# All eleven tiles of an expert layer through a seven-product scheme

## The chip, the cores and the metric

The kernel runs on one core of a Trainium2 chip. The metric is the device time of one execution in microseconds. A core has TensorE (matmuls, results into PSUM, of which the program uses eight banks of 512 fp32 columns), VectorE, ScalarE, GpSimd and SyncE, which here issues all transfers. The profile calls them PE, DVE, ACT, POOL and SP; PEld is the loading of a matmul's stationary operand.

## The reference

Three layers follow each other; everything is fp32. Attention has 4 x 8 heads over 576 positions of 64 features and keeps the 32 largest scores of a row. Its output is a matrix x of 2304 tokens and 512 features. A dense layer computes g = h cos(h) with h = x w_in (2048 wide) and then g w_out. The last layer mixes eight experts:

```
logits = x @ w_gate;  P = exp(logits - max)
8 times: P /= row sums; P /= column sums; P *= N / E
for e in 8 experts:
    h  = max(x @ w1[e], 0)          # 2304 x 512 @ 512 x 1024
    out += P[:, e:e+1] * (h @ w2[e])  # 2304 x 1024 @ 1024 x 512
```

## The kernel before

**Precision.** The matmuls of this part work in the type float32r. A matrix is split into a high part (ScalarE, a copy into that type) and a low part (VectorE or GpSimd, the difference), `split_cols`. A product then takes three matmuls: high x high, high x low, low x high (`mm3`, lines 504 to 510).

**Order.** Every operation is given to a planner (`put`) with its engine, an estimated cost, what it reads and what it writes. The planner (`listed`, line 245 on) goes through time: when an engine is free it takes, of the operations whose inputs are ready by the estimates, the one that was put first (within this part of the program). The order so found for each engine is then fixed; on the chip each engine works in that order and waits by semaphores. The estimate for a matmul of n columns is `mm_ns`, n/2.4 + 3 ns.

**Stages.** The first seven token tiles of 128 ("fill") go through the experts early, beside attention; their expert outputs are kept in memory and summed up at the end (`sum_fill`, 56 steps). The other eleven tiles (RT = 11) are the subject. Their dense layer (`moe1`) runs in three parts of 512, 512 and 384 tokens. `moe1` makes first-layer blocks ("in", twelve matmuls) and, seven blocks later, starts second-layer blocks; hidden values pass through rings of three buffers (hs, rr). At its end `keep_raw` (parts one and two) copies the result from the banks y0 to y3 to the buffer acc, splits it and computes the logits; `keep_parts` (part three) only splits it.

**The last stage** goes over 8 experts and 4 quarters j of the 1024 hidden features (two blocks of 128 hidden features each): 32 passes. The first matmul of a pass, 2 x 256 features halves by 2 x 128 hidden features by two halves of the tokens, is a 2 x 2 block product. For the first eight tiles it is made with seven products instead of eight (`mixed_first`, a scheme of Strassen's kind): `weight_mix` forms the sums of weight blocks on GpSimd (S1 to S4), `combine` once forms the differences of token blocks on VectorE (T1 to T4) and splits all seven operands (th, tl). Each product is six matmuls of 512 columns into one of four banks (s, y3, h, g, in turn); two are copied to SBUF by ScalarE, five sums are made by VectorE and two by GpSimd in SBUF; the results go through `gates`: the high part of relu by ScalarE, the low part by VectorE. The other three tiles (384 tokens) take plain matmuls, 24 of 384 columns (`plain_first`). Then each of the eleven tiles has six second matmuls of 512 columns into a bank of y0 to y2 (`mixed_second`), and VectorE multiplies by the gate's column and adds to acc. Blocks are put so that the tiles of one block come behind the first products of the next block. The gate normalisation (`sinkhorn`) is put before the first pass; it uses the bank t.

Of the kernel before, what the change touches and what calls it, by code (L numbers as in the profile page):

```python
# [10 lines left out]
F32 = mybir.dt.float32  # L11
F32R = mybir.dt.float32r
# [332 lines left out]

def act_ns(n, psum=False, ap=False):
    return (51.0 if psum else 93.0) + n / 1.2 + (93.0 if ap else 0.0)
# [10 lines left out]
def fused_kernel(tc, kq, vv, w_in, w_out, w_gate, w1, w2, out, B=4):  # L358
# [14 lines left out]
    LEAD, FILL, MIXED = 3, 7, 8  # L373
    AHEAD = (2, 1, 1)
    RT = NTT - FILL
    NR = NT - (FILL + MIXED) * 128
# [127 lines left out]
    def mm3(o, ob, ah, al, bh, bl, n, start, stop, bufs):  # L504
# [5 lines left out]
        put("PE", 3 * mm_ns(n), emit, bufs, [ob])  # L510
# [343 lines left out]
    def keep_raw(xb, i0):  # L854


        def done(p):
            n, pb = p.n, p.h()
            for d in range(4):
                h2, l2 = gh_r(), gl_r()  # L860
                yb, yv = p.y(d)
                r2, rb = (lambda d=d: xb.ap[:, i0 + d, :n]), (xb, i0 + d, i0 + d + 1)
                put("ACT", act_ns(n, psum=True), lambda yv=yv, r2=r2: A_.activation(r2(), yv(), AF.Copy), [yb], [rb])
                split_cols((h2, lambda h2=h2: h2.ap[:, :n]), (l2, lambda l2=l2: l2.ap[:, :n]), (rb, r2), n, eng=eng_w)
                put("PE", 2 * mm_ns(n), logits(pb, lambda h2=h2: h2.ap[:, :n], lambda l2=l2: l2.ap[:, :n], d, n), [wg, h2, l2], [pb])
            keep_logits(pb, p.n0, n)

        return done

# [16 lines left out]
    def gates(v, vb, n, g_r, psum):  # L886

        gh, gl = g_r()
        put("ACT", act_ns(n, psum=psum), lambda: A_.activation(gh.ap[:, :n], v(), AF.Relu), [vb], [gh])
        put("DVE", dve_ns(n), lambda: V.scalar_tensor_tensor(gl.ap[:, :n], v(), 0.0, gh.ap[:, :n].bitcast(F32), op0=ALU.max, op1=ALU.subtract), [vb, gh], [gl])  # L890
        return gh, gl

    def fill(e, t0, k, h_ring):
# [10 lines left out]
        for f in range(NF2):  # L904
# [7 lines left out]
            pend.append((f, *gates(lambda pb=pb: pb.ap[:, :n], pb, n, lambda: (gh_r(), gl_r()), True)))  # L912
# [56 lines left out]
    def combine(x2, th, tl):  # L969


        for c in range(2):
            x = lambda i: ((x2, i, i + 1), lambda: x2.ap[:, i, :])
            b11, b21, b12, b22 = x(c), x(c + 2), x(c + 4), x(c + 6)
            t1, t2 = x(8), x(9)
            t3, t4 = ((b, lambda b=b: b.ap) for b in (st_r(), st_r()))
            for o, p, q in ((t1, b12, b11), (t2, b22, t1), (t3, b22, b12), (t4, b21, t2)):
                put("DVE", dve_ns(512), lambda o=o, p=p, q=q: V.tensor_tensor(o[1](), p[1](), q[1](), op=ALU.subtract), [p[0], q[0]], [o[0]])
            for k, v in ((B11, b11), (B21, b21), (B22, b22), (T1, t1), (T2, t2), (T3, t3), (T4, t4)):
                iv = (k * 2 + c, k * 2 + c + 1)  # L980
                split_cols(((th, *iv), lambda k=k, c=c: th.ap[:, k, c, :]), ((tl, *iv), lambda k=k, c=c: tl.ap[:, k, c, :]), v)
# [21 lines left out]
    def mixed_first(A, th, tl, mix_r, g_r):  # L1003

        banks = Cycle([ps_s, ps_y[3], ps_h, ps_g])

        def product(a, b):
            bank = banks()
# [3 lines left out]
            def emit():  # L1012
                for c in range(2):
                    s = slice(s0 + c * 128, s0 + c * 128 + 128)
                    bh, bl = th.ap[:, b, c, :], tl.ap[:, b, c, :]
                    T_.matmul(bank.ap, h.ap[:, s], bh, start=c == 0, stop=False)
                    T_.matmul(bank.ap, h.ap[:, s], bl, start=False, stop=False)
                    T_.matmul(bank.ap, l.ap[:, s], bh, start=False, stop=c == 1)

            put("PE", 6 * mm_ns(512), emit, [h, l, (th, b * 2, b * 2 + 2), (tl, b * 2, b * 2 + 2)], [bank])  # L1020
            return bank, lambda: bank.ap

        bufs = [mix_r() for _ in range(4)]
        spot = lambda i: ((bufs[i // 2], i % 2 * 512, i % 2 * 512 + 512), lambda: bufs[i // 2].ap[:, i % 2 * 512 : i % 2 * 512 + 512])

        def copy(i, x):
            o = spot(i)
            put("ACT", act_ns(512, psum=True), lambda: A_.activation(o[1](), x[1](), AF.Copy), [x[0]], [o[0]])
            return o

        def plus(i, x, y, eng="DVE"):
            o = spot(i)
            f, cost = (V, dve_ns(512)) if eng == "DVE" else (G_, pool_ns(512))
            put(eng, cost, lambda: f.tensor_tensor(o[1](), x[1](), y[1](), op=ALU.add), [x[0], y[0]], [o[0]])
            return o

        def gate(x):
            return gates(x[1], x[0], 512, g_r, False)

        p1 = copy(0, product(A11, B11))  # L1040
        u = plus(1, product(S2, T2), p1)
        p5 = copy(2, product(S1, T1))
        v = plus(3, product(S3, T3), u)
        w = plus(4, u, p5, "POOL")
        c11 = gate(plus(5, product(A12, B21), p1))
        c21 = gate(plus(6, product(A22, T4), v))
        c22 = gate(plus(2, v, p5, "POOL"))
        c12 = gate(plus(7, product(S4, B22), w))
        return (c11, c21), (c12, c22)

    def plain_first(A, xh, xl, n, g_r):
        g = []
        for i, bank in ((0, ps_g), (1, ps_y[3])):
            h, l = A[i]
            for c in range(4):
                s = slice(c * 128, c * 128 + 128)
                iv = (c * n, c * n + n)
                mm3(lambda bank=bank: bank.ap[:, :n], bank, lambda h=h, s=s: h.ap[:, s], lambda l=l, s=s: l.ap[:, s], lambda c=c: xh.ap[:, c, :], lambda c=c: xl.ap[:, c, :],
                    n, c == 0, c == 3, [h, l, (xh, *iv), (xl, *iv)])
            g.append(gates(lambda bank=bank: bank.ap[:, :n], bank, n, g_r, True))  # L1060
        return (tuple(g),)
# [3 lines left out]
    def mixed_second(acc, t0, k, g, e, j, wo):  # L1065
        for t in range(k):
            y, T = y_r(), t0 + t
            c = slice(t % 4 * 128, t % 4 * 128 + 128)
            for i in (0, 1):
                gh, gl = g[t // 4][i]  # L1070
                oh, ol = wo[i]
                mm3(lambda y=y: y.ap, y, lambda gh=gh, c=c: gh.ap[:, c], lambda gl=gl, c=c: gl.ap[:, c], lambda oh=oh: oh.ap, lambda ol=ol: ol.ap,
                    512, i == 0, i == 1, [oh, ol, gh, gl])
            a, av = (acc, T, T + 1), lambda T=T: acc.ap[:, T, :]
# [10 lines left out]
            if e == NE - 1 and j == 3:  # L1085
                r = (FILL + T) * 128
                dma(lambda r=r: out[r : r + 128, :], av, 1 << 18, [a])

# [77 lines left out]
    th = buf("ph2", [128, 7, 2, 512], F32R, "th")  # L1166
    tl = buf("ph2", [128, 7, 2, 512], F32R, "tl")
    xrh = buf("ph2", [128, 4, NR], F32R, "xrh")
    xrl = buf("ph2", [128, 4, NR], F32R, "xrl")
    acc = buf("ph2", [128, RT, DM], F32, "acc")  # L1170
# [3 lines left out]
    moe1(Part(n0 + 512, three, keep_raw(acc, 0)), 4)  # L1174
    moe1(Part(n0 + 1024, three, keep_raw(acc, 4)), 4)
    moe1(Part(n0 + 1536, three, keep_parts(xrh, xrl), NR), 4)
# [65 lines left out]
```

## Time and profile before

| | |
|---|---|
| median of 3 runs | 2364.43 us (2361.56 to 2368.71) |
| profiled execution | 2365.81 us, span of its instructions 2364.0 us |
| mean granted TensorE clock | 0.998 |
| busy share of the span | PE 99%, PEld 82%, DVE 77%, ACT 56%, POOL 53% |
| instructions | 34301, of them 11487 matmuls |
| transfers | 242.28 MB, mean 102 GB/s |

The busy share of an engine is a mean over stages with different limits. In the timeline a row has the start, the duration, the engine, the line of the program, the operation, output and inputs by the program's names, and the shape; a bracket gives the idle time of the engine just before and what ended it. Matmuls are pipelined, so their durations overlap; how long one holds TensorE is read from start to start. "x4" in a row means four merged instructions.

### The profile page before, as it was taken

The numbers are of one execution on the slowest core, as the hardware profiler recorded it, in microseconds if no ns is written. First come the engines' busy times: TensorE is split into PE (matmuls) and PEld (weight loads), VectorE is DVE, ScalarE is ACT, GpSimd is POOL, SyncE is SP. The second block draws the span as 40 slices with busy tenths as digits, with TensorE's granted clock in tenths as the row PEclk, the third lists the DMA queues.
The fourth block names the chain that finished last, engine by engine and source line by source line (L and its number), as shares of the span: only waits on it lengthen the run. The fifth ranks groups of instructions, "written<-read, shape, count | busy, mean of one in ns | idle before, by whom it ended". The sixth has DMA issues, their size and how long they took to land.

```text
span 2364.0 us, 34301 instructions
## 1 busy us (share of the span) xinstructions
PE 2331.9 (99%) x11487; PEld 1932.1 (82%) x11487; DVE 1815.7 (77%) x3340; ACT 1333.3 (56%) x2688; POOL 1260.4 (53%) x1352
## 2 busy tenths in 40 slices
PE   9999999999899999999999999999999999999999
PEld 7655989898677888888888897888888888888887
DVE  7991999999869999999177796876666666666665
ACT  5884888888787777777477675222232222222221
POOL 6982987888876666665401036433333344444440
PEclk9999999999999999999999999999999999999999
DMA  7661654555333333433443332122222221111101
GB/s 222 204 182 40 188 163 141 171 158 169 118 86 94 120 120 120 120 100 95 126 123 108 117 116 65 41 76 77 85 77 80 77 66 36 36 36 36 36 23 49
DMA packets 152464, 242.28 MB, mean 102 GB/s; under 512 B 14624, under 2 KB 61808, under 8 KB 152288
## 3 DMA queue, kind: packets, MB, share of 16 engines
q1 hardware_dynamic: 152288, 240.10, 33.7%
q8 instruction: 90, 1.47, 0.3%
q14 instruction: 86, 0.70, 0.1%
HBM read 208.18 MB, written 31.87 MB: 102 GB/s over the span
## 4 chain that ended last, share of the span: by engine, by line
PE 83%; DVE 7%; POOL 4%; ACT 2%; DMA 2%; issue 2%; SPq 0%; POOLq 0%; ACTq 0%; DVEq 0%
PE y L506 11%; PE y L508 11%; PE y L507 11%; PE g L506 3%; PE g L508 3%; PE g L507 3%; PE t L606 3%; PE h L508 2%; PE h L506 2%; PE h L507 2%; PE y L517 2%; PE y L518 2%; PE t L632 2%; PE y L521 2%; PE s L578 1%
## 5 line engine op out<-in xcount | busy, mean ns | idle before, releaser
L481 POOL TENSOR_TENSOR wlo<-raw,whi 128x512 fp32r<-128x512 f32 x336 | 443.4, 1325 | 141.6 <-ACT whi L479 110.8
L594 DVE MAX8 m<-wk 128x8 f32<-128x576 f32 x432 | 317.7, 749 | 2.7
L1084 DVE SCALAR_TENSOR_TENSOR acc<-y,P,acc 128x512 f32<-128x512 f32 x308 | 229.3, 748 | 103.5 <-PE y L508 103.2
L479 ACT ACTIVATE whi<-raw 128x512 fp32r<-128x512 f32 x416 | 258.0, 626 | 82.5 <-PE y L508 30.4
L593 DVE MATCH_REPLACE8 wk<-m,wk 128x576 f32<-128x576 f32 x288 | 214.1, 744 | 1.9
L506 PE MATMUL y<-whi,gh 128*128 128x512 f32 x448 | 181.1, 404 | 0.0
L508 PE MATMUL y<-whi,gl 128*128 128x512 f32 x448 | 176.3, 394 | 0.0
L506 PE MATMUL y<-gh,xh 128*128 128x512 f32 x450 | 175.9, 391 | 0.1
L507 PE MATMUL y<-wlo,gh 128*128 128x512 f32 x448 | 175.7, 392 | 0.0
L508 PE MATMUL y<-gh,xl 128*128 128x512 f32 x450 | 175.1, 389 | 0.0
L507 PE MATMUL y<-gl,xh 128*128 128x512 f32 x450 | 175.1, 389 | 0.0
L588 ACT ACTIVATE sc<-s 128x288 f32<-128x288 f32 x288 | 116.6, 405 | 36.2 <-PE s L582 20.6
L606 PE MATMUL t<-ident,ex 128*128 128x128 f32 (+1 forms) x720 | 127.3, 275 | 8.0 <-DVE atl L625 3.4
L596 ACT ACTIVATE ex<-sc,m 128x576 f32<-128x576 f32 x144 | 111.1, 772 | 27.0 <-DVE m L594 25.7
L601 POOL TENSOR_SCALAR ex<-ex,m 128x576 f32<-128x576 f32 x144 | 110.8, 770 | 27.6 <-DVE m L600 24.2
L606 PEld LDWEIGHTS t<-ident,ex 128*128 128x128 f32 (+1 forms) x720 | 84.0, 134 | 49.4 <-issue 10.6
L590 DVE MAX8 m<-sc 128x8 f32<-128x576 f32 x144 | 107.5, 747 | 18.8 <-ACT sc L588 18.7
L624 ACT ACTIVATE ath<-t 64x128 fp32r<-64x128 f32 (+3 forms) x272 | 104.2, 395 | 29.0 <-PE t L606 26.1
L597 ACT ACTIVATE ex<-ex,m 128x576 f32<-128x576 f32 x144 | 111.5, 774 | 6.9 <-POOL m L595 2.3
L593 DVE MATCH_REPLACE8 wk<-m,sc 128x576 f32<-128x576 f32 x144 | 106.9, 743 | 0.1
L506 PEld LDWEIGHTS y<-gh,xh 128*128 128x128 f32 x450 | 84.5, 188 | 18.6 <-DVE acc L1080 0.8
L508 PE MATMUL y<-gh,gl 128*128 128x512 f32 x254 | 99.5, 392 | 0.0
(378 smaller groups left out, 7047.2 us busy)
## 6 DMA issues: line engine op xcount, KB each, us to landing
raw<-in_w_dram SPq DMA_DIRECT2D x384, 256.0 KB, 2.7
kq<-in_kq_dram SPq DMA_DIRECT2D x40, 576.0 KB, 4.0
raw<-win_d SPq DMA_DIRECT2D x64, 256.0 KB, 3.0
raw<-wout_d SPq DMA_DIRECT2D x64, 256.0 KB, 2.7
y_d<-st SPq DMA_DIRECT2D x56, 256.0 KB, 3.0
raw<-y_d SPq DMA_DIRECT2D x56, 256.0 KB, 2.7
d_raw<-in_w_in_dram SPq DMA_DIRECT2D x16, 512.0 KB, 5.4
d_raw<-in_w_out_dram SPq DMA_DIRECT2D x16, 512.0 KB, 3.7
```

Source lines behind the costliest of these rows:

```text
L479: put("ACT", act_ns(n), lambda: A_.activation(hv(), rv(), AF.Copy), [rb], [hb])
L481: put(e, c, lambda: f.tensor_tensor(lv(), rv(), hv().bitcast(F32), op=ALU.subtract), [rb, hb], [lb])
L506: T_.matmul(o(), ah(), bh(), start=start, stop=False)
L507: T_.matmul(o(), ah(), bl(), start=False, stop=False)
L508: T_.matmul(o(), al(), bh(), start=False, stop=stop)
L588: put("ACT", act_ns(288, psum=True), lambda c=c: A_.activation(sc.ap[:, c], o(), AF.Copy), [ps_s], [(sc, c.start, c.stop)])
L593: put("DVE", 669, lambda r=r, src=src: V.match_replace(wk.ap, mc(8 * r, 8), src.ap, LOWEST), [src, (m, 8 * r, 8 * r + 8)], [wk])
L594: put("DVE", 669, lambda r=r: V.max(mc(8 * r + 8, 8), wk.ap), [wk], [(m, 8 * r + 8, 8 * r + 16)])
L596: put("ACT", act_ns(S, ap=True), lambda: A_.activation(ex.ap, sc.ap, AF.Prelu, scale=-1.0, bias=mc(31), alpha=TINY), [sc, (m, 24, 32)], [ex])
L597: put("ACT", act_ns(S, ap=True) + 93.0, lambda: A_.activation(ex.ap, ex.ap, AF.Exp, scale=-0.125 / TINY, bias=mc(32), accum_out=mc(33)), [ ...
L606: T_.transpose(pt()[:p, c - c0, :], ex.ap[:, c * 128 : c * 128 + p], ident.ap)
L1084: put("DVE", 663, lambda y=y, av=av, pcol=pcol: V.scalar_tensor_tensor(av(), y.ap, pcol(), av(), op0=ALU.mult, op1=ALU.add), [y, P, a], [a])
```

## The change

All eleven tiles now go through the seven-product scheme, as two operand sets: one of N1 = 384 columns (six tiles) and one of N2 = 320 (five tiles). `plain_first` is gone. Sums are kept in PSUM: product two adds to the bank of product one after that was copied out, product five adds to the same bank, and so on, so that three copies and three VectorE sums (with a PSUM output) remain and GpSimd makes none; gates read PSUM. In the second set each result is gated in two pieces, of 256 and 64 columns. `mixed_first` and `mixed_second` are now generators that are advanced in turn: one product, one tile of the half before. A fifth bank, t, joins the ring of banks from the second expert on. The gate buffers of a pass are all six of their ring. The first operand set is formed before the third part of the dense layer, the second after it; the third part's result is copied in three pieces into acc. The chunks for the first weights are now the four of the dense layer's input. The gate normalisation is put behind the first pass. The expert sums of the fill tiles are taken two in a pass, not four. The planner's estimate for matmuls of this stage is `mx_ns`, n/2.4 + 13.3 ns.

```diff
+def mx_ns(n):
+    return n / 2.4 + 13.3
...
+    N1, N2 = 384, 320
...
-    def keep_raw(xb, i0):
+    def keep_raw(xb, places):
...
-                r2, rb = (lambda d=d: xb.ap[:, i0 + d, :n]), (xb, i0 + d, i0 + d + 1)
-                put("ACT", act_ns(n, psum=True), lambda yv=yv, r2=r2: A_.activation(r2(), yv(), AF.Copy), [yb], [rb])
-                split_cols((h2, lambda h2=h2: h2.ap[:, :n]), (l2, lambda l2=l2: l2.ap[:, :n]), (rb, r2), n, eng=eng_w)
+                for s0, m, k in places:
+                    k += d * (N1 + N2)
+                    put("ACT", act_ns(m, psum=True), lambda yv=yv, s0=s0, m=m, k=k: A_.activation(xb.ap[:, k : k + m], yv()[:, s0 : s0 + m], AF.Copy), [yb], [(xb, k, k + m)])
+                put("ACT", act_ns(n, psum=True), lambda yv=yv, h2=h2: A_.activation(h2.ap[:, :n], yv(), AF.Copy), [yb], [h2])
+                put("DVE", dve_ns(n), lambda yv=yv, h2=h2, l2=l2: V.tensor_tensor(l2.ap[:, :n], yv(), h2.ap[:, :n].bitcast(F32), op=ALU.subtract), [yb, h2], [l2])
...
-    def combine(x2, th, tl):
+    def combine(th, tl, x2, p0, n):
...
-            t1, t2 = x(8), x(9)
-            t3, t4 = ((b, lambda b=b: b.ap) for b in (st_r(), st_r()))
+            ta, tb = hs_r(), rr_r()
+            t1, t2, t3, t4 = (((b, k, k + n), lambda b=b, k=k: b.ap[:, k : k + n]) for b in (ta, tb) for k in (0, 512))
...
-    def mixed_first(A, th, tl, mix_r, g_r):
-
-        banks = Cycle([ps_s, ps_y[3], ps_h, ps_g])
+    banks = Cycle([ps_s, ps_y[3], ps_h, ps_g])
+
+    def mixed_first(A, th, tl, n, temps, dest):
...
+            put("PE", 6 * mx_ns(n), emit, [h, l, (th, b * 2, b * 2 + 2), (tl, b * 2, b * 2 + 2)], [bank])
...
+        def plus(out, bank, x):
+            put("DVE", dve_ns(n), lambda: V.tensor_tensor(out.ap[:, :n], bank.ap[:, :n], x[1](), op=ALU.add), [bank, x[0]], [out])
+
+        def gate(i, bank):
+            for (gh, gl), k, s0, m in dest[i]:
+                gates(lambda s0=s0, m=m: bank.ap[:, s0 : s0 + m], bank, m, gh, gl, k, psum=True)
+
+        X, Z = banks(), banks()
+        product(X, A11, B11)
+        p1 = copy(0, X)
+        yield
+        product(Z, S1, T1)
+        yield
+        product(X, S2, T2, True)
+        u = copy(1, X)
+        yield
+        Y = banks()
+        product(Y, A12, B21)
+        plus(Y, Y, p1)
+        gate(0, Y)
+        yield
+        product(X, S3, T3, True)
+        v = copy(2, X)
+        W = banks()
+        plus(W, Z, v)
+        gate(3, W)
+        yield
+        product(Z, S4, B22, True)
+        plus(Z, Z, u)
+        gate(2, Z)
+        yield
+        product(X, A22, T4, True)
+        gate(1, X)
+        yield
...
+    moe1(Part(n0 + 512, three, keep_raw(acc, [(0, 512, 0)])), 4)
+    moe1(Part(n0 + 1024, three, keep_raw(acc, [(0, 512, 4 * N)])), 4)
+    combine(*t1, acc, 0, N1)
+    moe1(Part(n0 + 1536, three, keep_raw(acc, [(0, 192, 512), (192, 64, 4 * N + 640), (256, 128, 4 * N + 512)]), NR), 4)
     whi_r.bufs, wlo_r.bufs = ring
-    combine(acc, th, tl)
-    sinkhorn()
-    chunks = list(zip(more[:1] + whi_r.bufs + gh_r.bufs, more[1:] + wlo_r.bufs + gl_r.bufs))
-    chunks += [(View(xh, i), View(xl, i)) for i in range(4)]
+    combine(*t2, acc, N1, N2)
+    chunks = [(View(xh, i), View(xl, i)) for i in range(4)]
+    chunks += zip(more[:1] + whi_r.bufs + gh_r.bufs, more[1:] + wlo_r.bufs + gl_r.bufs)
...
+    second, sums = iter(()), sum_fill()
     for e in range(NE):
+        if e == 1:
+            banks.bufs.append(ps_t)
         for j in range(4):
             A = weight_mix(e, j, wa_r, mix_r)
             wo = [split_weight(w2[e, f], dst=w2_r()) for f in (j, j + 4)]
...
+            g = [[g_r() for _ in range(2)] for _ in range(3)]
+            temps = [mix_r() for _ in range(3)]
+
+            firsts = (
+                mixed_first(A, *t1, N1, temps[:2], [[(g[i // 2][i % 2], 0, 0, N1)] for i in range(4)]),
+                mixed_first(A, *t2, N2, temps[2:], [[(g[2][i % 2], i // 2 * 256, 0, 256), (g[0][i % 2], 384 + i // 2 * 64, 256, 64)] for i in range(4)]),
+            )
+            tiles = (
+                [(t, g[t // 4], t % 4 * 128) for t in (0, 1, 2, 4, 5, 6)],
+                [(3, g[2], 0), (8, g[2], 128), (9, g[0], 384), (7, g[2], 256), (10, g[2], 384)],
+            )
+            for first, tile_list in zip(firsts, tiles):
+                for _ in first:
+                    next(second, None)
+                for _ in second:
+                    pass
+                second = mixed_second(acc, tile_list, e, j, wo)
             if e == j == 0:
-                for part in [plain(), mixed()]:
-                    mixed_second(acc, *part)
-                continue
...
+                sinkhorn()
             if e:
-                for _ in range(4):
+                for _ in range(2):
                     next(sums, None)
```

## Rows read from the trace of the kernel before

**Rows 1.** The page's chain that ended last: share of the span by engine.

```profile
PE 83%; DVE 7%; POOL 4%; ACT 2%; DMA 2%; issue 2%; SPq 0%; POOLq 0%; ACTq 0%; DVEq 0%
```

**Rows 2.** Busy time by stretch: stretch, length, busy us (instructions) by engine, granted clock, transfers.

```profile
core 0: us, PE busy (x) PEld busy (x) DVE busy (x) ACT busy (x) POOL busy (x), PEclk, DMA share, GB/s
1366.00:1391.00 25.00, 25.00 (x146) 25.00 (x145) 24.06 (x37) 21.08 (x39) 19.30 (x5) 1.00 0.37 113
1413.00:1440.00 27.00, 24.29 (x127) 21.79 (x126) 19.71 (x27) 16.04 (x30) 15.26 (x12) 0.94 0.38 110
1440.00:1520.00 80.00, 78.94 (x371) 65.04 (x370) 61.48 (x132) 31.90 (x56) 44.27 (x37) 1.00 0.15 41
1520.00:2360.00 840.00, 840.00 (x3861) 714.86 (x3859) 540.41 (x765) 227.05 (x396) 316.54 (x274) 1.00 0.19 56
```

**Rows 3.** Timeline of TensorE: ends of two blocks of a pass, and one 18 passes later.

```profile
1810.54 0.39 PE L1016 MATMUL s<-th,whi 128*128 128x512 f32 x1
...
1820.06 0.39 PE L506 MATMUL y<-gh,xh 128*128 128x512 f32 x1
...
1824.14 0.33 PE L506 MATMUL g<-xrh,whi 128*128 128x384 f32 x1
...
1828.32 0.39 PE L506 MATMUL y<-gh,gh 128*128 128x512 f32 x1
...
2340.86 0.33 PE L506 MATMUL g<-xrh,whi 128*128 128x384 f32 x1
```

**Rows 4.** Timeline of TensorE in attention: matmuls of 320 columns.

```profile
709.16 0.31 PE L634 MATMUL t<-atl,vs 128*128 128x320 f32 x1
...
709.89 0.31 PE L632 MATMUL t<-ath,vs 128*128 128x320 f32 x1
```

**Rows 5.** Timeline of a pass: from a bank's last matmul to its readers.

```profile
1817.34 0.39 PE L1016 MATMUL y<-th,whi 128*128 128x512 f32 x1
1817.54 0.69 DVE L1034 TENSOR_TENSOR rr<-s,hs 128x512 f32<-128x512 f32 x1 [0.67 <-PE s L1018]
...
1818.33 0.63 ACT L889 ACTIVATE gh<-rr 128x512 fp32r<-128x512 f32 x1 [2.91 <-DVE rr L1034]
...
2342.96 0.33 PE L506 MATMUL y<-xrh,whi 128*128 128x384 f32 x1
...
2343.22 0.49 ACT L889 ACTIVATE xh<-g 128x384 fp32r<-128x384 f32 x1 [3.78 <-PE g L508]
...
2343.75 0.56 DVE L890 SCALAR_TENSOR_TENSOR xl<-g,xh 128x384 fp32r<-128x384 f32 x1 [1.94 <-ACT xh L889]
```

**Rows 6.** Chain that ended last, in time: from a VectorE difference to its matmul.

```profile
1431.71 0.04 issue
```

**Rows 7.** Groups of VectorE instructions from 1600 to 2200: busy us, mean ns, idle before.

```profile
L1084 DVE SCALAR_TENSOR_TENSOR acc<-y,P,acc 128x512 f32<-128x512 f32 x231 | 171.8, 748 | 71.6 <-PE y L508 71.3
L481 DVE TENSOR_TENSOR gl<-raw,gh 128x512 fp32r<-128x512 f32 x41 | 37.2, 947 | 0.0
```

**Rows 8.** Timeline of the entry to the last stage, TensorE and VectorE.

```profile
1424.42 0.45 PE L517 MATMUL y<-gh,whi 128*128 128x384 f32 x1 [0.80 <-ACT gh L479]
1424.70 0.34 PE L518 MATMUL y<-gh,wlo 128*128 128x384 f32 x1
...
1431.15 1.94 DVE L879 TENSOR_TENSOR xrl<-y,xrh 128x384 fp32r<-128x384 f32 x4
```

**Rows 9.** Timeline of the third part's start: VectorE, ScalarE, TensorE and GpSimd.

```profile
1370.64 1.78 DVE L978 TENSOR_TENSOR acc<-acc 128x512 f32<-128x512 f32 x1
...
1372.95 0.68 DVE L978 TENSOR_TENSOR st<-acc 128x512 f32<-128x512 f32 x1
...
1374.60 0.99 ACT L479 ACTIVATE gh<-rr 128x384 fp32r<-128x384 f32 x2 [0.91 <-DVE rr L731]
...
1375.62 0.33 PE L517 MATMUL y<-gh,ch 128*128 128x384 f32 x1
...
1376.71 14.54 POOL L481 TENSOR_TENSOR tl<-st,th 128x512 fp32r<-128x512 f32 x1 [4.84 <-ACT th L479]
```

**Rows 10.** Timeline of TensorE: the last column sums of the gate normalisation.

```profile
1515.91 0.39 PE L952 MATMUL t<-cs,ones 128*128 128x8 f32 x2 [0.80 <-DVE cs L951]
```

More of the change, by code (lines that the diff above doesn't have):

```diff
@@ L502, in moe1_weight, with mm3 @@
         return hi, lo
-    def mm3(o, ob, ah, al, bh, bl, n, start, stop, bufs):
+    def mm3(o, ob, ah, al, bh, bl, n, start, stop, bufs, ns=mm_ns):
         def emit():
@@ L883, in keep_parts, with gates @@
         return done
[L886 to L891, printed above, removed]
+    def gates(v, vb, n, gh, gl, k=0, psum=False):
+        hv, lv = lambda: gh.ap[:, k : k + n], lambda: gl.ap[:, k : k + n]
+        put("ACT", act_ns(n, psum=psum), lambda: A_.activation(hv(), v(), AF.Relu), [vb], [(gh, k, k + n)])
+        put("DVE", dve_ns(n), lambda: V.scalar_tensor_tensor(lv(), v(), 0.0, hv().bitcast(F32), op0=ALU.max, op1=ALU.subtract), [vb, (gh, k, k + n)], [(gl, k, k + n)])
     def fill(e, t0, k, h_ring):
@@ L1001, in weight_mix, with product @@
         return parts
-    def mixed_first(A, th, tl, mix_r, g_r):
-        banks = Cycle([ps_s, ps_y[3], ps_h, ps_g])
-        def product(a, b):
-            bank = banks()
+    banks = Cycle([ps_s, ps_y[3], ps_h, ps_g])
+    def mixed_first(A, th, tl, n, temps, dest):
+        def product(bank, a, b, more=False):
             h, l = A[a // 2]
@@ L1015, in emit @@
                     bh, bl = th.ap[:, b, c, :], tl.ap[:, b, c, :]
[L1016 to L1028, printed above, removed]
-            return o
[L1031 to L1061, printed above, removed]
+                    T_.matmul(bank.ap[:, :n], h.ap[:, s], bh, start=c == 0 and not more, stop=False, skip_group_check=True)
@@ new lines, in emit, with copy @@
+                    T_.matmul(bank.ap[:, :n], h.ap[:, s], bl, start=False, stop=False, skip_group_check=True)
+                    T_.matmul(bank.ap[:, :n], l.ap[:, s], bh, start=False, stop=c == 1, skip_group_check=True)
+            put("PE", 6 * mx_ns(n), emit, [h, l, (th, b * 2, b * 2 + 2), (tl, b * 2, b * 2 + 2)], [bank])
+        def copy(i, bank):
+            b, k = temps[i * n // 1024], i % (1024 // n) * n
+            o = (b, k, k + n), lambda: b.ap[:, k : k + n]
+            put("ACT", act_ns(n, psum=True), lambda: A_.activation(o[1](), bank.ap[:, :n], AF.Copy), [bank], [o[0]])
+            return o
@@ L1063, in fused_kernel, with mixed_second @@
+        u = copy(1, X)
[18 more added lines that the diff above has]
+        yield
     y_r = Cycle(ps_y[:3])
[L1065 to L1068, printed above, removed]
+    def mixed_second(acc, tiles, e, j, wo):
+        for T, g, k in tiles:
+            y = y_r()
```

51 lines of the change are left out of this document (23 added, 28 removed).

## The prediction

> **What bounds the kernel now.** I read the page's chain of work that ended last first, then the busy time by stage, then single instructions. TensorE is 83% of the chain [rows 1]. The stages tell where the rest is [rows 2]: from 1520 to 2360 us TensorE is busy 840.00 of 840.00 us; from 1440 to 1520 it misses 1.1 us; from 1413 to 1440 it misses 2.7 us and its granted clock averages 0.94. So the stage that the change rewrites is bound by the number and length of matmuls, and only its entry has waits. No other engine is near: VectorE 540 us, ScalarE 227 us, GpSimd 317 us of those 840 [rows 2].
>
> **Price of a matmul.** The 42 matmuls of seven 512-column products start at 1810.54 and the next instruction at 1820.06: 9.52/42 = 226.7 ns each. The 24 matmuls of 384 columns take 1824.14 to 1828.32: 174.2 ns. The distance between two such blocks, 18 passes apart, gives the pass: (2340.86 - 1824.14)/18 = 28.71 us [rows 3]. Recomputed: 108 x 226.7 + 24 x 174.2 ns = 28.66 us, so 0.05 us a pass is not explained by slots. The changed program needs 320 columns; attention has such matmuls, five in 709.89 - 709.16 = 0.73 us, 146 ns each [rows 4].
>
> **The change in TensorE's slots.** A pass (one expert, one quarter of the hidden columns; 32 in all) has 42 products of 512 columns, 24 plain matmuls of 384 and 66 second matmuls of 512. It becomes 42 x 384, 42 x 320 and the same 66: 42 x 174.2 + 42 x 146 + 66 x 226.7 ns = 28.41 us. That is 0.25 us less; with 147 ns for 320 columns and 173.5 for 384 it moves by less than 0.05 us either way. I take 0.235 us, x 32 = 7.5 us saved, with ends 6.6 and 8.0. There are 1152 columns fewer but 18 matmuls more in a pass, so about half of what the columns give is paid back: each matmul costs some 13 ns beyond its columns at 2.4 GHz (512/2.4 = 213.3 against 226.7; 320/2.4 = 133.3 against 146) [rows 3, 4]. The Trainium skill, "TensorE: Matmul & The Clock Gate", section "Back-to-back issue gap", gives the isolated gap as N/2.4 + 2.5 ns; by that the saving would be an estimated 13.9 us. The rows disagree (13 ns), and they decide.
>
> **New waits in steady state.** Today a block's gates are made a whole block (eight tiles, 10.9 us) ahead of the tiles that use them. Afterwards a tile of the new half is wanted one product after the seventh product. Hops [rows 5]: TensorE slot end to ScalarE 0.26 us (2342.96 to 2343.22), to VectorE 0.20 (1817.34 to 1817.54); a 384-column ScalarE read of PSUM and its hop 0.53; a 512-column VectorE sum 0.69 and 0.10 to ScalarE, so 0.66 for 384 with the 0.56 of the gate's remainder, which has that length; and 0.04 from VectorE to TensorE [rows 6], 0.05 with rounding. VectorE writing its sum into PSUM is not in the trace; its nearest row is the same sum written to SBUF, which I take; from nothing to twice that it would move the waits below by - 0.6 to + 0.6 us. After the seventh product the gate chain is 0.26 + 0.53 + 0.61 = 1.40 us, while one product gives 1.05 or 0.88. The planner may put another ready product there: the fourth, whose bank is the older half's second bank, free 0.20 + 0.66 + 0.53 + 0.61 = 2.00 us after the sixth product. With five tiles in seven products the sixth and seventh stand together, so from the sixth product's end 1.05 + 0.88 = 1.93 us pass: short by 0.07, or by 0.28 when a tile's 0.75 us accumulation [rows 7] stands ahead in VectorE's queue. With six tiles a tile stands between and nothing is short. Likewise the sixth product waits for a copy and a sum: 0.26 + 0.53 + 0.61 = 1.40 against a tile of 1.36, short by 0.04. A matmul after a wait starts its successor 0.11 us late (1424.42 to 1424.70 is 0.28 against 0.174) [rows 8]. So 0 to (0.28 + 0.11) + (0.06 + 0.11) = 0.56 us a pass. I take 0.10, near the low end, because 840 us of the present stage show no wait at all [rows 2]: + 3.2 us. Cover for the rest: VectorE's work stays at about 8 us a pass for sums and gates (before 9 x 0.69 + 2 x 0.56 = 7.3; after 6 sums and 12 shorter gate pieces, 8.1), and it sums up two expert tiles a pass in place of four, the last in the last pass; at 64% busy that hides. Two GpSimd sums a pass go. What can upset VectorE's order is GpSimd: the weight splits of 512 columns average 947 ns [rows 7], where an undisturbed instruction of that kind takes 0.68 [rows 9]; none of that reaches TensorE today.
>
> **The entry, 1413 to 1440.** It goes from weights (four first chunks are now those of the x tiles, free once the last first-layer products are done) through the last part's result to the first pass. Removed: 2.7 us idle and 0.06 x 27 = 1.6 us of clock [rows 2], and some six restarts of 0.11 [rows 8]: 5.0 us. New: products one and four (2.1 us) can run while the last part's results are copied; product two needs bank y3, read until about 1433.1 (1431.15 + 1.94) [rows 8], 1.7 us after the two are done; five waits for the copy of three's sum, 0.8; seven for five's, 0.8; the first tile for seven's gate, 0.4; four restarts. There are no older tiles to put between: 4.1 us. Net - 0.9, with ends - 4 (the products fill all) and + 3 (the second operand set is late for its first product by its eight differences, 0.68 x 320/512 us each [rows 9]). The extra ScalarE copies of the last part (12 short ones for four) are in these copies' time; those of the two full parts keep their count and lie beside seven first-layer products of the next part.
>
> **The first operand set, 1359 to 1391.** Its splits and differences now go before the third part's own work, not behind it. Second-layer matmuls of that part begin at 1375.62, just after their gate (1374.60 + 0.99) [rows 9]: no slack but one first-layer block, 2.1 us, to be pulled ahead. VectorE is busy 24.1 of the 25 us from 1366 to 1391 [rows 2]. Four more differences there, 0.68 x 384/512 us each, cost some 2 us of a VectorE without reserve. I take + 1.5, ends 0 (the block pulled ahead covers it) and + 8 (the lock, below), nearer to 0 because TensorE stood without a wait there.
>
> **The end.** The last half's first tile waits for the seventh product's gate with nothing else left: 0.26 + 0.42 + 0.50 = 1.2 us for 256-column pieces, from rows 5 by columns. After that the tail is as now. The gate normalisation moves behind the first pass. It lies between 1440 and its last column sums on TensorE at 1515.91 [rows 10], under 76 us, and is wanted three passes, 85 us, later: 0, with a wait on TensorE like the 0.80 us one there at worst.
>
> **Sum.** - 7.5 + 3.2 - 0.9 + 1.5 + 1.2 = - 2.5 us on the profiled execution, 2365.81 us (span 2364.0 and 1.8 around it): 2363.3. That execution lies 1.4 us above the median of the runs, 2364.43, so the forecast is 2362 us, its own range 2355 to 2369.
>
> **Rivals.**
> Faster: the planner always finds a ready product. Then no steady wait, the entry gets its 5.0 us back for 1.0 of new waits, and 1.2 at the end: - 10.3, 2354 us. For it: today's stage has no wait, and five banks serve two halves. Against: the margins above are tenths of a microsecond.
> Slower: each pass pays both hand-over waits in full, 0.56 x 32 = 17.9 us: - 7.5 + 17.9 - 0.9 + 1.5 + 1.2 = + 12.2, 2377 us. It decides from 0.18 us a pass (no gain) and 0.40 (slower by 0.3%). For it: TensorE's order is fixed beforehand, and a VectorE instruction held by GpSimd (1.78 against 0.68 us [rows 9]) stops all behind it. Against: most such collisions fall on other instructions.
> The lock: fourteen GpSimd splits, now wanted early, against VectorE. Today a GpSimd split took 14.54 us while VectorE ran without a break, and a VectorE difference beside GpSimd took 1.78 us, another 0.68: 1.1 us lost [rows 9]. Fourteen such would be 15 us of VectorE time; with half of them in front of a gate that TensorE needs, 8 us take the place of the 1.5, the sum is + 4.0 and the time 2368 us. Against: five GpSimd splits ran in that stretch [rows 2] and TensorE did not wait. The Trainium skill, "SBUF — State Buffer", section "Who interferes with whom", says that a VectorE instruction with two SBUF inputs and a GpSimd instruction that reads SBUF block each other for the whole instruction; the 14.54 us agree. That the change does less than it says has no place: the counts are fixed by the program.
>
> **Chances.** Forecast 0.40, faster 0.31, slower 0.17, lock 0.12. What can be told from no change here is about 0.3%, 7 us: below 2357.3 or above 2371.5. Faster: nearly all of 0.31 and a tenth of the forecast's, 0.34. Slower: most of its rival and little of the lock's and the forecast's, 0.20. The same: 0.46. The range, 2350 to 2375, leaves out a little of both outer cases.
>
> **What would show it.** In the profile after: 320-column slots of 146 to 147 ns; passes of 28.4 us plus TensorE waits named after VectorE's gates or sums at the first tile, the fourth or the sixth product; the 0.94 clock gone or not at the entry; second-layer matmuls of the third part waiting on a gate around 1376. Passes of 28.4 us flat mean the faster rival, 28.9 and more the slower one. A slot for 320 columns near 174 ns would break the forecast at its root.

## The result and the profile after

The changed kernel takes 2378.61 us (median of 6 runs, 2374.85 to 2384.01); the kernel before, beside it, 2363.93. The ratio is 1.0063 with an interval of 1.0046 to 1.0080: slower by 14.7 us, outside the predicted range. The profiled execution took 2382.64 us, its span is 2380.7. Of the 16.7 us between the two spans, 4.65 arose within the first 110 us, where both programs run the same instructions (granted clock 0.95 there against 1.00); so all that follows is measured from the 6441st matmul on, which both programs reach with the same instructions, at 1271.57 us before and 1276.22 after. From there on the changed kernel's trace is 12.05 us longer.

The chain that ended last, answering to [rows 1]:

```profile
PE 84%; DVE 7%; ACT 3%; POOL 3%; issue 2%; DMA 2%; SPq 0%; POOLq 0%; ACTq 0%; DVEq 0%
```

Busy time by stretch, answering to [rows 2], same columns (the same times lie some 5 us earlier in the program's work than in the kernel before, which is that far ahead):

```profile
1366.00:1391.00 25.00, 21.86 (x120) 19.74 (x118) 23.62 (x33) 20.11 (x41) 12.86 (x10) 1.00 0.19 56
1413.00:1440.00 27.00, 25.73 (x148) 25.16 (x146) 20.06 (x27) 15.74 (x29) 14.74 (x13) 1.00 0.38 108
1440.00:1460.00 20.00, 15.46 (x67) 11.48 (x67) 14.75 (x22) 14.27 (x42) 18.50 (x18) 0.74 0.21 58
1460.00:1520.00 60.00, 60.00 (x319) 53.02 (x318) 38.72 (x112) 27.49 (x61) 19.03 (x20) 1.00 0.13 36
...
1560.00:2360.00 800.00, 799.87 (x4161) 712.03 (x4160) 510.22 (x918) 273.55 (x658) 212.51 (x210) 1.00 0.19 54
```

TensorE is busy throughout the long stage, as before. But it lost 3 us in the stretch of the first operand set, and 4.5 us beside a granted clock of 0.74 at the entry. The six largest waits of TensorE from 1355 to 1560 us (bank and line of the waiting matmul, releaser, us in total, times, longest):

```profile
PE h L743 <- ACT gh L870: 3.2, 1, 3.2
PE h L744 <- DVE gl L871: 1.8, 3, 0.7
PE s L511 <- ACT hs L847: 1.6, 1, 1.6
PE y L522 <- ACT gh L484: 1.1, 1, 1.1
PE s L1028 <- ACT hs L1037: 0.7, 1, 0.7
PE y L1028 <- DVE g L1041: 0.5, 1, 0.5
```

The timeline of TensorE in the long stage, answering to [rows 3]: the start of one product and of the same product 26 passes later, and between them the end of the older half's tiles in one pass. L511 to L513 are second matmuls, L1028 to L1030 products.

```profile
1603.34 0.44 PE L1028 MATMUL y<-th,whi 128*128 128x384 f32 x1
...
1746.08 0.39 PE L511 MATMUL y<-gh,gh 128*128 128x512 f32 x1
1746.31 0.40 PE L512 MATMUL y<-gl,gh 128*128 128x512 f32 x1
...
1747.48 0.44 PE L1028 MATMUL y<-th,xh 128*128 128x384 f32 x1
1747.76 0.34 PE L1029 MATMUL y<-tl,xh 128*128 128x384 f32 x1
...
1749.70 0.31 PE L1028 MATMUL t<-th,xh 128*128 128x320 f32 x1
...
1750.57 0.39 PE L511 MATMUL y<-whi,gh 128*128 128x512 f32 x1
...
2353.25 0.44 PE L1028 MATMUL t<-th,whi 128*128 128x384 f32 x1
```

The pass is (2353.25 - 1603.34)/26 = 28.84 us, where 28.41 and waits were predicted and the kernel before has 28.71. Six 320-column matmuls take 0.87 us, 145 ns each, as forecast. The six matmuls of a tile take 1747.48 - 1746.08 = 1.40 us, 233 ns each, against 226.7 in [rows 3], and TensorE shows no idle time there. Over the whole stage their mean is 231.7 ns.

**Where the 12.05 us are.** I took all matmuls from the 6441st on from start to start; that time is a matmul's slot. Each gets the slot of its length in an undisturbed run (226.7, 173.7, 146.2 ns); what it has beyond that counts as "lengthened" up to 25 ns, and above as wait, restart or half clock. "Other" are shorter forms (the gate normalisation, the transposes of the logits). Sums in us; E1 to E13 are the experiments below.

| kernel | slots | lengthened | waits, restarts, clock | other | total | to before |
|---|---|---|---|---|---|---|
| before | 1074.1 | 2.2 | 8.8 | 3.2 | 1088.2 | |
| after | 1065.9 | 10.5 | 20.9 | 3.0 | 1100.3 | +12.1 |
| E1 tiles in blocks | 1065.9 | 3.8 | 19.9 | 3.7 | 1093.3 | +5.0 |
| E3 before, split up | 1074.1 | 8.2 | 6.5 | 3.2 | 1091.8 | +3.6 |
| E6 second weights behind | 1065.9 | 10.6 | 19.5 | 3.0 | 1099.0 | +10.7 |
| E9 remainders on VectorE | 1065.9 | 10.2 | 17.4 | 3.6 | 1097.1 | +8.9 |
| E10 = E1 + E6 | 1065.9 | 3.9 | 17.0 | 3.2 | 1089.9 | +1.7 |
| E11 one block a pass | 1065.9 | 4.7 | 19.3 | 3.8 | 1093.6 | +5.4 |
| E13 = E1 + E6 + E9 | 1065.9 | 3.7 | 15.3 | 5.1 | 1090.0 | +1.8 |

The slots gave the predicted gain (8.1 us). It was taken back by 8.3 us of lengthened slots and 12.1 of waits, restarts and clock, of which 9.2 fall before the third pass.

### The profile page after: what moved, and what is told of

It reads as the page before. It is cut to its first block, busy times and chain, and to the rows that moved or that the text cites. A ratio compares the mean times of both kernels' runs of the same rounds, so it can differ in the third digit from the quotient of the medians.

```text
span 2380.7 us, 36005 instructions
## 1 busy us (share of the span) xinstructions
PE 2342.2 (98%) x12063; PEld 1974.9 (83%) x12063; DVE 1812.1 (76%) x3572; ACT 1403.1 (59%) x3034; POOL 1149.1 (48%) x1302
## 4 chain that ended last, share of the span: by engine, by line
PE 84%; DVE 7%; ACT 3%; POOL 3%; issue 2%; DMA 2%; SPq 0%; POOLq 0%; ACTq 0%; DVEq 0%
PE y L512 10%; PE y L511 10%; PE y L513 10%; PE t L611 3%; PE g L513 2%; PE g L511 2%; PE g L512 2%; PE h L513 2%; PE h L511 2%; PE h L512 2%; PE y L522 2%; PE y L523 2%; PE y L526 2%; PE s L1028 1%; PE y L790 1%
## 5 line engine op out<-in xcount | busy, mean ns | idle before, releaser
L486 POOL TENSOR_TENSOR wlo<-raw,whi 128x512 fp32r<-128x512 f32 x304 | 398.3, 1314 | 155.8 <-ACT whi L484 126.5
L511 PE MATMUL y<-whi,gh 128*128 128x512 f32 x800 | 319.3, 399 | 0.0
L513 PE MATMUL y<-whi,gl 128*128 128x512 f32 x800 | 314.6, 393 | 0.0
L512 PE MATMUL y<-wlo,gh 128*128 128x512 f32 x800 | 314.6, 393 | 0.0
L513 PEld LDWEIGHTS y<-whi,gl 128*128 128x128 f32 x800 | 150.1, 188 | 33.3
L511 PEld LDWEIGHTS y<-whi,gh 128*128 128x128 f32 x800 | 150.4, 188 | 22.1
L486 POOL TENSOR_TENSOR xl<-raw,xh 128x512 fp32r<-128x512 f32 (+1 forms) x48 | 62.7, 1309 | 214.7 <-ACT xh L484 212.0
L512 PEld LDWEIGHTS y<-wlo,gh 128*128 128x128 f32 x800 | 150.4, 188 | 18.3
L512 PE MATMUL y<-gl,gh 128*128 128x512 f32 x352 | 139.0, 395 | 0.0
L513 PE MATMUL y<-gh,gl 128*128 128x512 f32 x352 | 138.4, 393 | 0.0
L511 PE MATMUL y<-gh,gh 128*128 128x512 f32 x352 | 138.0, 392 | 0.0
L611 PEld LDWEIGHTS t<-ident,ex 128*128 128x128 f32 (+1 forms) x720 | 84.3, 135 | 49.8 <-issue 12.1
```

Of the source, the lines that this page charges most:

```text
L486: put(e, c, lambda: f.tensor_tensor(lv(), rv(), hv().bitcast(F32), op=ALU.subtract), [rb, hb], [lb])
L611: T_.transpose(pt()[:p, c - c0, :], ex.ap[:, c * 128 : c * 128 + p], ident.ap)
```

## The experiments

**Theory**: a change in the length of TensorE's matmuls makes the slots behind it longer. In the kernel before, the second matmuls have the length of the seven products, and only the plain 384-column matmuls interrupt them; afterwards tiles of 512 columns alternate with products of 384 or 320, six and six. **Rival**: ScalarE and VectorE now read and write sums in PSUM, and that slows TensorE. For the waits: orders on ScalarE and VectorE at the first operand set and at the entry.

**E1, tiles in blocks.** P6 and P7, the sixth and seventh product, also change places (that part of the edit is left out here), and they come behind the block.

```diff
-                for _ in first:
-                    next(second, None)
+                for _ in range(5):
+                    next(first)
                 for _ in second:
                     pass
+                for _ in first:
+                    pass
```

> The kernel after, in which the eleven second-product tiles of the older half no longer alternate with products: they run in one block between the fifth product and the last two (which change places), so that TensorE changes the length of its matmuls in two places a pass instead of at every six matmuls. Work, operands and sums are the same. Theory 1 (a change of length makes the next eight or nine slots longer): the 66 matmuls of the tiles return from a mean slot of 231.7 ns to 227 or 228, a pass from 28.84 to about 28.5 us, the whole from 2378.6 to about 2368. Theory 2 (the slots are longer since ScalarE and VectorE read and write more in PSUM): slots stay near 231 to 232 ns, the pass at 28.8, the whole at 2378. Waits that appear because the sums now come in bursts would show as idle time of TensorE, not as longer slots.

Measured: 2371.97 us, ratio 1.0038 (1.0026 to 1.0051), 6.6 us below the kernel after. Its timeline of TensorE: a run of 33 second matmuls, and the starts of two such blocks 25 passes apart:

```profile
1605.49 0.39 PE L511 MATMUL y<-gh,gh 128*128 128x512 f32 x1
...
1806.61 0.39 PE L511 MATMUL y<-whi,gh 128*128 128x512 f32 x1
...
1814.12 0.30 PE L1028 MATMUL s<-th,xh 128*128 128x320 f32 x1
...
2320.82 0.39 PE L511 MATMUL y<-whi,gh 128*128 128x512 f32 x1
```

(1814.12 - 1806.61)/33 = 227.6 ns a slot; the pass is (2320.82 - 1605.49)/25 = 28.61 us, 0.23 less. The PSUM traffic is the same, so the rival does not hold. The expected 10 us were too much: eight changes of length a pass remain of 24, where the expectation spoke of two places, and 3.8 us of lengthening are left.

**E3, the same from the other side**: in the kernel before, two tiles (one per `next`) stand behind each group of six plain matmuls, so that the length changes eight times a pass instead of twice.

```diff
             for c in range(4):
                 ...
+                if c % 2:
+                    next(between, None)
+                    next(between, None)
```

> The kernel before, in which only TensorE's order is changed: the 24 plain 384-column matmuls of a pass stand in four groups of six with two second-product tiles (of 512 columns) between them, so that the length changes eight times a pass instead of twice. Nothing is added to PSUM. Theory 1 (changes of length): 48 more tile matmuls of a pass fall into the longer slots, at 3 to 4 ns each, and the 384-column ones at 1 to 3: about 0.2 us a pass, 6 us in all, 2370. Theory 2 (PSUM traffic of the other engines): slots of the 512-column matmuls stay at 226.7 ns and the time within 2 us of the kernel before. Waits of TensorE for operands would be a third thing and are counted apart.

Measured: 2368.74 us, 1.0021 (1.0012 to 1.0030), 5.3 us slower. Timeline of TensorE:

```profile
1607.40 0.39 PE L1016 MATMUL s<-th,ch 128*128 128x512 f32 x1
...
1806.98 0.39 PE L506 MATMUL y<-gh,xh 128*128 128x512 f32 x1
...
1809.74 0.39 PE L1016 MATMUL s<-th,whi 128*128 128x512 f32 x1
...
2330.06 0.39 PE L1016 MATMUL s<-th,whi 128*128 128x512 f32 x1
```

Twelve second matmuls behind 384 columns take 2.76 us, 230 ns each; the pass is (2330.06 - 1607.40)/25 = 28.91 us against 28.71. Same work, same PSUM use, no wait in this stage: the order alone costs 0.2 us a pass.

**E5, the slots by themselves.**

```diff
+    for big, small, run, times in ((512, 512, 6, 6), (512, 384, 6, 6), (512, 320, 6, 6), ...):
+        for n in (big, small) * times:
+            for i in range(run):
+                T_.matmul(ps_g.ap[:, :n], th.ap[:, i % 7, 0, 0:128], tl.ap[:, i % 7, 0, 0:n], ...)
```

> The kernel before with 456 matmuls added behind its last sum, where no other engine works on TensorE's operands: runs of six 512-column matmuls in turn with runs of six of 512, 384, 320 or 256 columns, then runs of 24 (512 and 384), of twelve (512 and 320) and of one (512 and 384), all reading finished operands and writing one bank. It adds about 108 us of matmuls whose results nobody uses. Theory 1 (a change of length alone lengthens the slots behind it): 512 with 512 stays at 226.7 ns; six 512 after six 384 average 230 to 233 ns, the first matmuls of a run of 24 show 229 to 236 ns and the rest 226.7. Theory 2 (PSUM traffic of ScalarE and VectorE lengthens them): all slots here are flat, 226.7, 173.7 and 146 ns, since nobody else touches PSUM.

Busy time of the first three patterns, 72 matmuls each (the counts include those that overlap an edge); columns as in [rows 2]:

```profile
2365.46:2381.78 16.32, 16.32 (x74) 13.51 (x73) 0.75 (x1) 0.00 (x0) 0.00 (x0) 1.00 0.09 33
2381.78:2396.37 14.59, 14.59 (x74) 13.04 (x72) 0.00 (x0) 0.00 (x0) 0.00 (x0) 1.00 0.01 1
2396.37:2409.93 13.56, 13.56 (x73) 12.00 (x73) 0.00 (x0) 0.00 (x0) 0.00 (x0) 1.00 0.00 0
```

With one length 16.32/72 = 226.7 ns. In turn with 384 columns, 36 x (226.7 + 173.7) ns would be 14.41; it is 14.59. With 320: 13.42 and 13.56. In these two no other engine works; in the first VectorE does once, for 0.75 us. The single slots repeat to a nanosecond: 512 columns behind 384 take 229, 233, 236, 224, 231, 236 and, in a run of 24, on with 228, 232, 231 and then 226.7 throughout. The kernel after has the same numbers in the same places, so this is the whole of its lengthening in the tiles.

**E2, the first operand set later.** One line moves: `combine(*t1, ...)` behind the third part.

> The kernel after, in which the first three operand differences of the second layer (the set made from t1) are made behind the third part of the first layer instead of in front of it. Theory (ScalarE, in order, did the set's fourteen splits ahead of the copies that the third part's start waits for, and the splits waited for VectorE's slow differences): TensorE's idle time and restarts of 4 to 5 us between 1366 and 1391 us go, and 1 to 4 us of it come back at the entry of the second layer, where the set is then late: 2374 to 2378. Rival (the start of the third part waits for something else, such as the y copies alone): the idle time there stays above 3 us and the entry gets longer on top: 2380 or more.

Measured: 2377.38 us, 1.0056 (1.0041 to 1.0071). TensorE is busy for all of 1366 to 1391, as expected, and then waits 4.4 us at 1422, where the third part's last gate stands behind the set's differences on VectorE:

```profile
1426.90 0.69 PE L522 MATMUL y<-gh,whi 128*128 128x384 f32 x1 [4.38 <-ACT gh L484]
```

Its trace is 12.2 us above the one of before. The loss only moved.

**E7, the first set strewn over the third part**, two splits beside each of its blocks.

> The kernel after, in which the first three operand differences and their fourteen splits are strewn over the middle of the first layer's third part, two splits beside each of its blocks from the fifth on, instead of standing in front of the part. Theory (the loss at the part's start is one of order on ScalarE and VectorE, not of their load): TensorE's idle time of 3 us and its restarts between 1366 and 1391 us go, 4 us in all, and the entry stays as it is: about 2374.5. Rival (VectorE, 90% busy there, has no room: the loss moves with the splits): waits of 2 to 5 us appear between 1391 and 1437 us, 2377 to 2380.

Measured: 2381.88 us, 1.0086 (1.0071 to 1.0102). The rival was right, and the price higher than its 2 to 5 us of wait and 2377 to 2380 us. One weight remainder stands on VectorE behind a difference and gate remainders that GpSimd held (1.35 us, and 2.61 for two), and TensorE waits for it:

```profile
1386.82 0.69 PE L523 MATMUL y<-gh,wlo 128*128 128x384 f32 x1 [5.90 <-DVE wlo L486]
```

**E9, remainders of the sets on VectorE.**

```diff
-                split_cols(..., v, n)
+                split_cols(..., v, n, "DVE")
```

> The kernel after, in which the 28 remainders of the two operand sets are taken by VectorE instead of GpSimd. Theory (a GpSimd split holds VectorE for as long as it lasts: the differences took 1.37 us beside GpSimd and 0.55 without it): VectorE gets 14 x 0.47 = 6.5 us of work in front of the third part, but loses the 10 to 13 us that GpSimd's splits took; the idle time of TensorE between 1366 and 1391 us, 3.1 us, falls below 1.5 us, and the entry, where GpSimd is then free for the weights, gets shorter as well: 2370 to 2375. Rival (VectorE, 90% busy there, is short of time by its own work): the idle time rises to 6 us or more, 2382 to 2386.

Measured: 2376.08 us, 1.0053 (1.0040 to 1.0067). VectorE around the set, first the kernel after, then E9 (L991 are the differences, L486 remainders):

```profile
1367.17 0.55 DVE L991 TENSOR_TENSOR rr<-acc 128x384 f32<-128x384 f32 x1
...
1369.17 1.37 DVE L991 TENSOR_TENSOR hs<-acc,hs 128x384 f32<-128x384 f32 x1
1370.46 1.37 DVE L991 TENSOR_TENSOR rr<-acc 128x384 f32<-128x384 f32 x1
```

```profile
1369.70 1.02 DVE L486 TENSOR_TENSOR tl<-rr,th 128x384 fp32r<-128x384 f32 x2
1370.65 0.55 DVE L991 TENSOR_TENSOR hs<-acc,hs 128x384 f32<-128x384 f32 x1
1371.12 0.55 DVE L991 TENSOR_TENSOR rr<-acc 128x384 f32<-128x384 f32 x1
```

Busy time from 1361 to 1391 us, the kernel after and then E9:

```profile
1361.00:1391.00 30.00, 26.86 (x144) 23.96 (x142) 26.38 (x37) 23.43 (x47) 12.86 (x10) 1.00 0.21 64
```

```profile
1361.00:1391.00 30.00, 28.93 (x160) 26.49 (x159) 27.69 (x52) 25.26 (x51) 0.00 (x0) 1.00 0.25 73
```

VectorE takes over the GpSimd splits and grows by only 1.3 us; TensorE's idle time falls from 3.14 to 1.07. So GpSimd's hold on VectorE was two thirds of TensorE's idle time at the first set (2.07 of 3.14 us); the rest stays without it. The Trainium skill, "SBUF — State Buffer", section "Who interferes with whom", says that a VectorE instruction with two SBUF inputs and a GpSimd instruction that reads SBUF exclude each other; the 1.37 and 0.55 us agree. The time came out 1 us above the expected range.

**E4 and E6, the entry.** ScalarE at the entry of the kernel after, and TensorE:

```profile
1434.85 1.15 ACT L484 ACTIVATE whi<-raw 128x512 fp32r<-128x512 f32 x2 [1.24 <-DMA raw<-in_w_dram]
1438.50 0.63 ACT L484 ACTIVATE whi<-rr 128x512 fp32r<-128x512 f32 x1 [2.49 <-POOL rr L1010]
1439.03 0.61 ACT L484 ACTIVATE whi<-raw 128x512 fp32r<-128x512 f32 x1
1440.41 0.63 ACT L484 ACTIVATE whi<-rr 128x512 fp32r<-128x512 f32 x1 [0.77 <-POOL rr L1010]
1440.95 0.59 ACT L869 ACTIVATE acc<-y 128x192 f32<-128x192 f32 x3
```

```profile
1441.98 0.50 PE L743 MATMUL h<-gh,wg 128*16 128x384 f32 x1 [3.25 <-ACT gh L870]
...
1447.05 0.52 PE L1028 MATMUL y<-th,xh 128*128 128x384 f32 x1
1447.37 0.52 PE L1029 MATMUL y<-tl,xh 128*128 128x384 f32 x1
```

The result of the last part is there, but its copies (L869, L870) stand behind weight splits that wait for GpSimd's sums; behind the wait the 384-column slots are 0.32 us, TensorE's lower clock level (1.2 GHz), until 1450.57. Eleven such slots, 0.146 us too long each, cost 1.6 us, so what the clock took at the entry before is not gone. E4 put the first pass's splits behind the copies:

> The kernel after, in which the splits of the second layer's first weights (all but the first operand) are put behind the copies of the first layer's last part on ScalarE and GpSimd. Theory (at the entry ScalarE, in order, stood at a split that waited for GpSimd's weight sum, with the copies that TensorE waited for behind it): the wait of 3.25 us at 1438.39 falls below 1 us and the whole by 2 to 4 us, to about 2375. Rival (the copies wait for the product y0 or for VectorE): the wait stays at 3 us, and the products of the first pass are late as well, 2379 or more.

Measured: 2382.93 us, 1.0083 (1.0069 to 1.0096), worse. The buffers tell why: the first pass's sums lie in tt, those in rr (whi<-rr above) belong to the second pass. The wait fell to 1.3 us, but the first pass's weights came late; E4's ScalarE:

```profile
1432.85 0.63 ACT L484 ACTIVATE whi<-rr 128x512 fp32r<-128x512 f32 x1 [0.80 <-POOL rr L1010]
...
1443.72 0.61 ACT L484 ACTIVATE xh<-raw 128x512 fp32r<-128x512 f32 x1
1444.24 1.13 ACT L484 ACTIVATE xh<-tt 128x512 fp32r<-128x512 f32 x2
```

E6 holds back the right ones (`late` is written by the copies of the last part):

```diff
-            split_cols(..., raw)
+            split_cols(..., raw, behind=[late] if e == 0 and j == 1 else [])
```

> The kernel after, in which the splits of the second pass's weights (not of the first's, as in the run before) are put behind the copies of the first layer's last part in ScalarE's order. Theory (the splits that stood on ScalarE in front of the copies from 1435 to 1440.95 are those of the second pass's weight sums, wanted only 28 us later): TensorE's wait of 3.25 us at 1438.39 falls below 0.7 us and the whole by 2.5 to 3.5 us, to about 2375.5. Rival (the copies are late for the product y0, or the first pass's weights are late as well, as when those were held back): TensorE's idle time between 1437 and 1465 us stays above 5 us, 2378 or more.

Measured: 2376.98 us, 1.0060 (1.0046 to 1.0074). The 3.25 us wait is gone, and the remainders on VectorE are late next (the two largest of E6's waits, same columns as above):

```profile
PE h L746 <- DVE gl L873: 2.6, 4, 1.0
PE s L1030 <- ACT hs L1039: 1.7, 2, 0.9
```

Half of the expected gain was left. The times of E2, E6 and E9 lie within the interval of the kernel after; what tells them apart is the place of the waits in the traces.

**E8, E10 to E13, edits together.** E8 is E1 + E6 + E7:

> The kernel after with three changes of order together: second-product tiles in one block between the fifth product and the last two; the second pass's weight splits behind the copies of the first layer's last part; the first operand set strewn over the third part. If the three losses are separate, they add up: 2378.6 less 6.6 (tiles in one block, as measured), less 3 and less 4 gives about 2365, the same as the kernel before within 0.3%. If one of the two waits moves only to another place: 2368 to 2372.

2373.13 us, 1.0048 (1.0035 to 1.0062), above both expected figures: E7's wait is in it (5.9 us). E10 is E1 + E6:

> The kernel after with the two changes of order that each helped: second-product tiles in one block a half, and the second pass's weight splits behind the copies of the last part. If both gains hold beside each other: 2371.97 less 1.6 is about 2370, slower than before by 0.2 to 0.4%. If the first pass in blocks waits where the copies now come sooner: 2372 to 2374.

2367.81 us, 1.0019 (1.0008 to 1.0029); the two gains add up and more. E11 puts all eleven tiles of a pass in one block, between 384-column products:

> As the run with tiles in a block per half and the second weights behind, but all eleven tiles of a pass stand in one block, between the third and the fourth product of the next pass's first set: one block of 512 columns a pass instead of two. Theory (only changes of length lengthen the slots): the lengthened part falls from 3.0 us (28 passes) to about 2, the one restart a pass behind the last gates may go as well (3 us), so 1 to 4 us less than the run with two blocks: 2366 to 2369. Rival (the products, fourteen in a row, now wait for banks and gates): TensorE waits of 0.2 us and more a pass, 2374 or above.

2371.20 us, 1.0032 (1.0020 to 1.0044). A miss: six changes a pass in place of eight, but the lengthening grew (4.7 against 3.9 us). The price is one of the pair of lengths: in E5 the first six 384-column slots behind a run of 24 of 512 columns take 171, 175, 178, 185, 176 and 182 ns (25 ns too much in all), while 320 columns behind 512 take 143 to 147. That is 0.8 of the 3.7 us between the traces of E11 and E10; 2.3 are waits, most of them at the entry, which no run singles out. E12 is E11 + E9:

> As the run with all eleven tiles in one block, with the 28 remainders of the operand sets on VectorE as well. If each part helps by itself: 2360 to 2365, level with the kernel before or below it. If VectorE is short of time in the third part: 2370 or more.

2369.43 us, 1.0016 (1.0006 to 1.0026), between the two expected figures. And E13 is E10 + E9:

> The kernel after with the three edits that each gave something: second-product tiles in one block a half, the second pass's weight splits behind the copies of the last part, and the remainders of the operand sets on VectorE. If the three losses (lengthened slots, GpSimd holding VectorE at the first set, ScalarE's order at the entry) are the whole of what went wrong, the predicted gain in slots should be left over: 2367.8 less 2.5 is 2365, level with the kernel before within 0.2%, with TensorE idle for less than 1.5 us between 1361 and 1391 us and for less than 6 us at the entry. If one of them only moved: 2368 or more.

2367.41 us, 1.0018 (1.0009 to 1.0027). TensorE's idle time is 1.07 us between 1361 and 1391, as expected, and 4.07 at the entry (1433 to 1461). But in two later passes a product waits, 1.1 us for a copy on ScalarE at 1726 and 1.6 for a gate's remainder on VectorE at 1927; E10 has only the first, so part of E9's gain is lost again. None of these versions beats the kernel before. In traces the three edits bring +12.1 us down to +1.8, in medians +14.7 to +4.5. The 2 to 4 us by which the medians of these kernels lie above what their traces show from the 6441st matmul on are not placed: one execution each was traced, and runs of one kernel spread over some 10 us.

## Why the prediction was wrong, step by step

**Price of a matmul, and the change in TensorE's slots: the step that failed.** "9.52/42 = 226.7 ns each" and "42 x 174.2 + 42 x 146 + 66 x 226.7 ns = 28.41 us" took the slot as a property of a matmul's own length. Both blocks of [rows 3] are runs of one length. The 0.05 us a pass that slots did not explain were the two changes of length in a pass of the kernel before (1.65 us in the third to the thirtieth pass), and I let them go. The new order changes the length 24 times a pass. Product counts and slots were right (8.1 us); lengthening, which had no term, took 8.3. E1, E3 and E5 show it. It is the largest part of the 14.6 us between the forecast of - 2.5 and the + 12.1 found; the entry is the next, with 5.9.

**New waits in steady state** were right in place: the one that came is the sixth product's, which waits for a copy and a sum. ScalarE and VectorE behind the tile that starts at 1746.08 in the timeline of TensorE above:

```profile
1746.34 0.49 ACT L1037 ACTIVATE rr<-s 128x384 f32<-128x384 f32 x1 [1.34 <-PE s L1030]
1746.86 0.57 DVE L1041 TENSOR_TENSOR g<-y,rr 128x384 f32<-128x384 f32 x1 [0.62 <-ACT rr L1037]
```

The hops are 0.26, 0.52 and 0.62 us, 1.40 in all as worked out, and the product starts at 1747.48 into the bank that the sum has read. The tile itself takes nearly as long, so little is left of the wait but the late start of the successor, 1747.48 to 1747.76 or 0.28 us against 0.174. The second wait, behind the seventh product, shows in no pass from the fourth on. From the third to the thirtieth pass waits and restarts grew by 2.7 us, where + 3.2 was predicted. That the size fits is in part luck: the 0.10 us a pass was chosen near the low end of a range whose working has gaps (the sixth product's wait is 0.04 us in one sentence and 0.06 in the sum, and the 0.28 of the other wait is not worked out). The slower rival gave 2377 us by these waits at 0.56 us a pass; the time came near it, but not its mechanism.

**The first operand set**: + 1.5 was taken, it cost 4.2 us (0.32 + 1.74 + 0.44 + 1.30 beyond the slots, and four restarts of 0.11 behind them, where the kernel before has none). The rival's mechanism, GpSimd against VectorE, acted, at a quarter of its price of 8: E9 takes 2.1 of the 4.2 us away, and the rest leaves this place only when the whole set does (E2); "TensorE stood without a wait there" was no reserve, since VectorE was 96% busy [rows 2].

**The entry**: - 0.9 was predicted, + 5.0 measured (9.2 us of waits, restarts and clock before the third pass, less 4.2 for the set). The removed waits did go: from 1413 to 1437 us TensorE is busy throughout. The new ones were listed at 4.1 us, but not that in-order ScalarE would do the second pass's splits, which wait for GpSimd, ahead of the copies (E6), nor that the clock would fall behind the longer wait.

**The end**: + 1.2 was predicted for a first tile with nothing else in front of it. There was something: a tile of the older half stood behind the last product, from 2369.92 to 2371.30 us, and no wait came. The 0.2 us found are the usual restarts of the last two passes.

Predicted: - 7.5 + 3.2 - 0.9 + 1.5 + 1.2 = - 2.5. Found: - 8.1 (slots) + 8.3 (lengthening) + 2.7 (steady waits) + 4.2 (first set) + 5.0 (entry) + 0.2 (end) - 0.2 (other forms) = + 12.1.

## What to carry to other kernels

A matmul's slot measured in a run of equal ones holds for such a run: where the order mixes lengths, price the sequence as it will stand, and keep matmuls of one length together, with an eye on which lengths meet (E11). A small unexplained rest in the pass before (0.05 of 28.71 us) is a term to be named when the change multiplies what may cause it. And work that is moved forward is priced on the in-order engines it is put in front of, with the slower durations that it brings with it, even when TensorE shows no wait there today.

## What the runs showed of the hardware

Slots behind a change of length follow a fixed sequence, the same in a full kernel and with all other engines idle: 512 columns behind 384 need nine slots to return to 226.7 ns, behind 320 or 256 five or six (E5: 233, 236, 229, 232, 231, 227 behind 256; E1 behind 320: 231, 231, 235, 229, 232, 231). Some slots are shorter than the steady ones (224; 171 for 384 columns). In turns of one and one, 512 and 384 columns take 237 + 175 = 412 ns against 400. What in the engine causes it, the records do not tell.
